# A gated linear attention with a feed-forward layer: a new order of steps, two sums moved from TensorE to VectorE, and a new layout of the feed-forward weights

## The chip, the core and the metric

The kernel runs on one core of one Trainium2 chip. The metric is the device time of one execution in microseconds (us). It is longer than the span from the first to the last instruction in the profile: 213.44 against 211.5 us for the profiled execution of the kernel before.

Ratios are computed as the mean time of one kernel's fast runs over the mean of the other's fast runs of the same rounds, on the same chip. So they are not quite the ratios of the medians that I quote. A run counts as slow here when it is over 1.5% above the fastest of its kernel; slow runs are left out of ratios.

## The reference

Four sequences of 768 tokens with 8 heads of 48 channels go through a recurrence with a decay for each channel and token. Its result, 3072 tokens of 384 features, goes through a normalised gated feed-forward layer with 1536 hidden units.

```python
for t in range(S):
    cur = np.einsum('bhd,bhe->bhde', u[None] * kt, vt)
    y[:, :, t] = np.einsum('bhd,bhde->bhe', rt, state + cur)
    state = wt[:, :, :, None] * state + np.einsum('bhd,bhe->bhde', kt, vt)
...
xn = x / rms * rms_g
g, val = xn @ w_gate, xn @ w_val
return (g * (1.0 / (1.0 + np.exp(-g))) * val) @ w_out
```

## The kernel before

The tokens are cut into six superblocks n of 128 tokens, each with four items j, one for each sequence. For each item the logarithms of the decays are summed along the tokens by a matmul with a triangular mask. The exponentials of two such sums scale r and k; then come matmuls for the scores (`q_mm`), the state (`st_mm`) and the output (`y_mm`). The feed-forward pass of superblock n (twelve steps of gate and value matmuls, then four output matmuls) is interleaved by hand with the attention of superblock n + 1. One long list, `ORDER`, gives the order of the steps. Every engine executes its share of this list in order.

```python
def cs_mm(n, j):                      # both decay sums on TensorE
    ...
    nc.tensor.matmul(a[:, NP:NP + DM]..., lhsT=mask_lt, rhs=rhs, start=True, stop=False)
    ...                               # four small matmuls: the total decay
    nc.tensor.matmul(b[:, 0:DM]..., lhsT=mask_nle, rhs=rhs, start=True, stop=True)

def st_mm(n, j):                      # the old state is added by a matmul with the identity
    old = n > 0 and n not in OLD_DVE  # OLD_DVE = () before
    if old:
        nc.tensor.matmul(ps..., lhsT=ident, rhs=st[:, n % 2, j]..., start=True, stop=False)
    for i in range(NP):
        nc.tensor.matmul(ps[:, i, :], lhsT=pair(rk[:, n % 2, j, 1], i), rhs=pair(vb[n, j], i), ...)

def load_wo(g, _):                    # one row of w_out per packet: 384 floats, cast to bf16
    ... in_=moe_w_out[...].rearrange("(c p) m -> p c m", p=128)

def fc_mm(ps, ws, n, f):              # dense slices of the gate and value weights
    for c in range(KC):
        nc.tensor.matmul(ps, lhsT=ws[:, c, f * 128:(f + 1) * 128], rhs=xnt[n][:, c, :], ...)
```

The gate matmuls and the first decay sum share two banks (`ps_a`) of PSUM, the memory that matmuls write to, the value matmuls and the second decay sum two others (`ps_b`). A matmul that needs a bank waits until its last reader is done; for `ps_b` that reader is an operation of VectorE (the multiply with k, or the product with the activated gate). In this way VectorE can hold up TensorE.

## Time and profile before

| | before |
|---|---|
| time, median of its first three runs | 212.09 us (211.61 to 215.77) |
| profiled execution | 213.44 us, span 211.5 us |
| TensorE busy | 194.5 us, 92% |
| VectorE busy | 147.6 us, 70% |
| stages 1 to 4 | 36.9, 31.8, 31.0, 28.9 us |

A stage is the stretch of the TensorE timeline from the first gate matmul of one superblock to that of the next. Before stage 1 comes a start-up of 29.3 us, after stage 4 a tail with the last two feed-forward passes. (The prediction takes the start of the fifth gate pass from the chain of waits, 158.06 us; the TensorE timeline has it at 157.90. So it gives stage 4 as 29.1 us; I use 28.9 from here on, and the tail is 53.6 us.)

### The profile page before, as it was taken

How to read it: one execution, taken by the hardware profiler on the slowest of the kernel's cores; microseconds unless marked ns; L12 is line 12 of the kernel's file. 1: busy time of each engine (PE TensorE's matmuls, PEld its weight loads, DVE VectorE, ACT ScalarE, POOL GpSimd, SP SyncE). 2: the span in 40 equal slices, each digit the busy share in tenths (PEclk: the TensorE clock that was granted, in tenths of full speed). 3: DMA queues.
4: the chain of work that ended last, by engine and by line, in shares of the span. 5: the costliest groups of instructions: out<-in, count | busy, mean ns of one | idle time of the engine just before them, and what ended most of it. 6: DMA issues, size and time to landing. Idle time of an engine off the chain costs nothing.

```text
span 211.5 us, 4381 instructions
## 1 busy us (share of the span) xinstructions
PE 194.5 (92%) x1534; PEld 107.7 (51%) x1552; DVE 147.6 (70%) x295; ACT 138.1 (65%) x282; POOL 108.6 (51%) x167
## 2 busy tenths in 40 slices
PE   5687779998998799999999999999999999999993
PEld 2455434455664245665455565455655544544563
DVE  6498744899876688988689799667886755235411
ACT  3796994769796356997546998578858873225300
POOL 3498402869597593699697889473222520000000
PEclk9999999999999999999999999999999999999999
DMA  6999999899999999999999999992177030000122
GB/s 131 217 217 183 171 203 211 169 201 168 194 205 188 190 186 228 219 213 192 192 195 222 230 222 124 236 188 48 56 186 127 20 76 20 37 0 37 40 111 76
DMA packets 126878, 32.41 MB, mean 153 GB/s; under 512 B 120580, under 2 KB 126088, under 8 KB 126856
## 3 DMA queue, kind: packets, MB, share of 16 engines
q1 hardware_dynamic: 123664, 28.58, 67.9%
q0 software_dynamic: 3184, 3.54, 10.4%
q8 instruction: 12, 0.20, 0.4%
q14 instruction: 10, 0.08, 0.1%
q10 hardware_dynamic: 8, 0.00, 0.0%
HBM read 25.96 MB, written 4.72 MB: 145 GB/s over the span
## 4 chain that ended last, share of the span: by engine, by line
PE 68%; DMA 7%; SPq 7%; DVE 6%; ACT 5%; issue 3%; POOL 3%; ACTq 0%; DVEq 0%; POOLq 0%
PE ps_b L546 20%; PE ps_a L546 19%; PE ps_q L606 18%; SPq L208 4%; DMA kt<-in_k_dram 3%; DMA vt<-in_v_dram 3%; PE ps_q L443 2%; SPq L221 2%; DMA xnt<-xn 2%; DVE ht L564 2%; PE ps_q L491 2%; PE ps_q L488 1%; DVE rk L402 1%; ACT junk L501 1%; PE ps_b L375 1%
## 5 line engine op out<-in xcount | busy, mean ns | idle before, releaser
L564 DVE TENSOR_TENSOR ht<-ps_b,sg 128x512 bf16<-128x512 f32 x72 | 48.7, 688 | 25.8 <-PE ps_b L546 18.6
L195 ACT ACTIVATE sg<-ps_a 128x512 bf16<-128x512 f32 x72 | 42.6, 596 | 36.3 <-PE ps_a L546 34.9
L546 PE MATMUL ps_b<-xnt,wv_sb 128*128 128x512 bf16 x208 | 58.6, 384 | 2.7 <-DVE rk L402 1.5
L546 PE MATMUL ps_a<-xnt,wg_sb 128*128 128x512 bf16 x206 | 58.8, 385 | 1.2 <-DVE wcol L394 0.6
L606 PE MATMUL ps_q<-wo_sb,ht 128*128 128x384 bf16 (+1 forms) x300 | 49.9, 319 | 0.0
L408 POOL TENSOR_TENSOR ruk<-rt,kt 128x384 f32<-128x384 f32 x24 | 24.3, 1011 | 25.5 <-DMA rt<-in_r_dram 20.2
L606 PEld LDWEIGHTS <-ht 128*128 128x128 bf16 x300 | 28.4, 98 | 16.9
L546 PEld LDWEIGHTS <-wv_sb 128*128 128x128 bf16 x216 | 20.2, 99 | 25.1 <-issue 4.9
L546 PEld LDWEIGHTS <-wg_sb 128*128 128x128 bf16 x216 | 20.2, 99 | 24.2 <-issue 1.7
L409 POOL TENSOR_TENSOR ruk<-ruk,u_bc 128x384 f32<-128x384 f32 x24 | 24.1, 1005 | 1.9
L418 POOL TENSOR_TENSOR ydiag<-vt,diag 128x384 f32<-128x384 f32 x24 | 19.8, 830 | 3.7 <-DVE diag L413 2.9
L461 POOL TENSOR_SCALAR_AFFINE_SELECT qts<-qts 128x512 bf16<-128x512 bf16 x20 | 12.6, 635 | 14.2 <-ACT qts L454 14.2
L450 DVE TENSOR_TENSOR qts<-ps_q,mask_lt 128x512 bf16<-128x512 f32 x24 | 16.2, 683 | 3.8 <-issue 2.5
L496 DVE TENSOR_TENSOR xb<-ps_q,ydiag 128x384 f32<-128x384 f32 x24 | 13.3, 552 | 5.3 <-PE ps_q L491 4.8
L195 ACT ACTIVATE lw<-wt 128x384 bf16<-128x384 f32 x24 | 12.0, 516 | 5.1 <-DMA wt<-in_w_dram 4.9
L514 ACT ACTIVATE xn<-xb,rstd 128x384 bf16<-128x384 f32 x24 | 14.4, 606 | 0.8 <-POOL rstd L510 0.8
L454 ACT CAST qts<-ps_q 128x512 bf16<-128x512 f32 x20 | 11.6, 584 | 4.7 <-PE ps_q L445 4.7
L501 ACT ACTIVATE junk<-xb 128x384 bf16<-128x384 f32 x24 | 12.4, 517 | 3.4 <-DVE xb L496 3.3
L402 DVE TENSOR_TENSOR rk<-kt,ps_b 128x384 bf16<-128x384 f32 x20 | 11.0, 549 | 5.1 <-ACT ps_b L195 3.0
L193 ACT ACT_TABLE_LOAD x10 | 12.8, 1283 | 1.8 <-PEq L642 1.6
L397 DVE TENSOR_TENSOR rk<-rt,ps_a 128x384 bf16<-128x384 f32 x20 | 11.0, 548 | 4.1 <-DMA rt<-in_r_dram 3.0
L615 ACT COPY ob<-ps_q 128x384 f32<-128x384 f32 (+1 forms) x12 | 5.5, 461 | 12.1 <-PE ps_q L606 11.4
(71 smaller groups left out, 271.6 us busy)
## 6 DMA issues: line engine op xcount, KB each, us to landing
wt<-in_w_dram SPq DMA_DIRECT2D x24, 192.0 KB, 3.7
vt<-in_v_dram SPq DMA_DIRECT2D x24, 192.0 KB, 4.2
kt<-in_k_dram SPq DMA_DIRECT2D x24, 192.0 KB, 3.8
rt<-in_r_dram SPq DMA_DIRECT2D x24, 192.0 KB, 3.8
out_dram<-ob SPq DMA_DIRECT2D x23, 192.0 KB, 2.8
wo_sb<-in_moe_w_out_dram POOLq DMA_DIRECT2D x3, 384.0 KB, 6.1
wv_sb<-in_moe_w_val_dram POOLq DMA_DIRECT2D x1, 768.0 KB, 10.6
wg_sb<-in_moe_w_gate_dram POOLq DMA_DIRECT2D x1, 768.0 KB, 14.0
```

Of the source, the lines that this page charges most:

```text
L195: return nc.scalar.activation(**kw).ins
L402: nc.vector.tensor_tensor(out=rk[:, n % 2, j, 1, :, 0:D], in0=inp["k", n, j], in1=bank["cs_k", n, j][:, 0:DM].rearrange("p (h d) -> p h d" ...
L408: nc.gpsimd.tensor_tensor(out=ruk[n, j], in0=inp["r", n, j], in1=inp["k", n, j], op=ALU.mult)
L409: nc.gpsimd.tensor_tensor(out=ruk[n, j], in0=ruk[n, j], in1=u_bc, op=ALU.mult)
L418: nc.gpsimd.tensor_tensor(out=ydiag[n, j], in0=inp["v", n, j], in1=diag[n, j].to_broadcast([128, H, D]), op=ALU.mult)
L450: nc.vector.tensor_tensor(out=qts[n, j][:, 0], in0=bank["q", n, j][0], in1=bc_mid(mask_lt, NP), op=ALU.mult)
L496: nc.vector.tensor_tensor(out=xb[n, j], in0=bank.pop(("y", n, j)), in1=ydiag[n, j].rearrange("p h d -> p (h d)"), op=ALU.add)
L501: nc.scalar.activation(out=junk, in_=xb[n, j], func=AF.Square, accum_out=rstd[n, j][:, 0:1])
L514: nc.scalar.activation(out=xn, in_=xb[n, j], func=AF.Copy, scale=rstd[n, j][:, 1:2])
L546: nc.tensor.matmul(ps, lhsT=ws[:, c, f * 128:(f + 1) * 128], rhs=xnt[n][:, c, :], start=(c == 0), stop=(c == KC - 1))
L564: nc.vector.tensor_tensor(out=ht[n][:, f, :], in0=bank.pop(("v", n, f)), in1=bank.pop(("sg", n, f)), op=ALU.mult)
L606: nc.tensor.matmul(ps[:, cols], lhsT=ht[n][:, f, b * L:(b + 1) * L], rhs=wo_sb[:, f, cols], start=(f == 0), stop=(f == FC - 1))
```

## The change

The intent is to take work from the fullest engine. The old state is added by VectorE in superblocks 2 to 4. The second decay sum is no longer a matmul: it is the first sum plus the logarithm itself, with the sign turned in the exponential, so one VectorE addition replaces it in superblocks 4 and 5. Each partition takes four neighbouring rows of the output weights, so that one packet carries 6144 bytes instead of 1536; the hidden units are then numbered in steps of four, and the gate and value weights are read with that stride. From superblock 1 on, the list of steps is a new one.

```diff
-    OLD_DVE = ()
+    OLD_DVE = (2, 3, 4)
+    ONE_SUM = (4, 5)
...
+        if n not in ONE_SUM:
+            nc.tensor.matmul(b[:, 0:DM]..., lhsT=mask_nle, rhs=rhs, start=True, stop=True)
+
+    def cs_add(n, j):
+        b = bank["cs_k", n, j] = psB.tile([128, 512], FP32, name="ps_b")
+        nc.vector.tensor_tensor(out=b[:, 0:DM]..., in0=bank["cs_r", n, j][:, NP:NP + DM]...,
+                                in1=lw[:, n % 2, j, :, 0:D], op=ALU.add)
...
-        act(LN_EXP, out=bank["cs_k", n, j][:, 0:DM], in_=ps, func=AF.Exp)
+        act(LN_EXP, out=bank["cs_k", n, j][:, 0:DM], in_=ps, func=AF.Exp, scale=-1.0 if n in ONE_SUM else 1.0)
...
-            in_=moe_w_out[...].rearrange("(c p) m -> p c m", p=128)
+            in_=moe_w_out[...].rearrange("(p c) m -> p c m", c=FG)
...
+    def units(ws, c, f):
+        ...
+        return ws[g][:, c, a:a + FG * 128].rearrange("p (m i) -> p i m", i=FG)[:, f % FG, :]
...
-            nc.tensor.matmul(ps, lhsT=ws[:, c, f * 128:(f + 1) * 128], rhs=xnt[n][:, c, :],
+            nc.tensor.matmul(ps, lhsT=units(ws, c, f), rhs=xnt[n][:, c, :],
...
-(ORDER: some 900 of its 1052 steps in another order)
+(ORDER: 1060 steps, the eight cs_add among them)
```

The gate and value weights also lie in one tile for each load instead of one for all, and some set-up instructions moved.

## The prediction

> **What bounds the kernel now.** I read the first page's busy shares and its 40-slice strip, then the timeline of TensorE, then the chain of work that ended last, then the timeline of VectorE. Page, busy time and strip (each digit is a fortieth, 5.3 us):
>
> ```profile
> PE 194.5 (92%) x1534; PEld 107.7 (51%) x1552; DVE 147.6 (70%) x295; ACT 138.1 (65%) x282; POOL 108.6 (51%) x167
> ...
> PE   5687779998998799999999999999999999999993
> ...
> DMA  6999999899999999999999999992177030000122
> ```
>
> TensorE is full from about 31 us to the end, apart from a dip in slice 13. The DMA engines are full until about 140 us: they fetch all inputs ahead. Which of the two sets the time has to be read stage by stage. A stage here runs from the first gate matmul of one superblock to that of the next. In the TensorE timeline the first gate matmuls stand at 29.3, 66.2, 98.0, 129.0 and 158.1 us, so stages 1 to 4 last 36.9, 31.8, 31.0 and 29.1 us; start-up is 29.3, the tail (the last two feed-forward passes) 53.4.
>
> Durations of matmuls overlap, so I take their cost from the distances between starts (timeline of TensorE: start, duration, instruction):
>
> ```profile
> 119.70 0.33 PE L370 MATMUL ps_a<-lw,mask_lt 128*128 128x384 bf16 x1
> 119.86 0.24 PE L373 MATMUL ps_a<-ones_col,lw 128*128 128x1 bf16 x4
> 119.96 0.32 PE L375 MATMUL ps_b<-lw,mask_nle 128*128 128x384 bf16 x1
> 120.12 2.11 PE L606 MATMUL ps_q<-wo_sb,ht 128*128 128x384 bf16 x12
> 122.07 0.33 PE L370 MATMUL ps_a<-lw,mask_lt 128*128 128x384 bf16 x1
> ...
> 128.29 0.32 PE L468 MATMUL ps_q<-st,ident 128*128 128x384 bf16 x1
> 128.46 0.33 PE L471 MATMUL ps_q<-vb,rk 128*128 128x96 bf16 x4
> ```
>
> The second decay-sum matmul (L375) holds the array for 120.12 - 119.96 = 0.16 us, the identity matmul that brings in the old state (L468) for 0.17, twelve output matmuls for 1.95, and the timeline gives 0.65 for three gate or value matmuls, 0.335 for the q matmuls of one item, 0.375 for the y, 0.17 for state and for the transposes of xn. Summing each stage's program order with these gives TensorE 32.4, 29.2, 30.6, 28.6 us in stages 1 to 4. The excess over the sums is 4.5, 2.6, 0.4 and 0.5: stages 3 and 4 are bound by TensorE, stage 2 has one hole. Of stage 1's excess some 2.3 us is matmuls at half pace between 30.1 and 34.1 us (0.43 each instead of 0.216), the rest small waits.
>
> The hole of stage 2, in the chain of work that ended last (start, us, what):
>
> ```profile
> 64.17 5.69 DMA kt<-in_k_dram
> 69.86 0.03 issue
> 69.89 0.02 DVEq L402
> 69.91 0.04 issue
> 69.95 0.57 DVE rk L402
> 70.52 0.04 issue
> 70.56 0.81 PE ps_b L546 x3
> ```
>
> The last k tile of superblock 2 lands at 69.9; its multiply frees a PSUM bank; the value matmul starts at 70.56. TensorE loses 1.7 us there and 0.75 just before (the r tile landed at 67.5, the gate matmul began at 68.2): 2.45 in all. Until there, DMA bandwidth bounds.
>
> VectorE timeline, where two operations of 384 columns follow without a wait:
>
> ```profile
> 126.59 0.54 DVE L397 TENSOR_TENSOR rk<-rt,ps_a 128x384 bf16<-128x384 f32 x1
> 127.05 0.55 DVE L402 TENSOR_TENSOR rk<-kt,ps_b 128x384 bf16<-128x384 f32 x1
> 127.51 1.11 DVE L536 TENSOR_TENSOR xnt<-ps_q,gT 128x384 bf16<-128x384 bf16 x2
> ```
>
> 0.55 us long, but 0.46 to 0.47 apart: VectorE overlaps them too, and its true load is below the 70% of the page. I use 0.475 for 384 columns and 0.61 for 512 (115.36 to 115.97 in the same view), 0.56 for the two state multiplies together.
>
> **What the Trainium skill says.** (1) "TensorE: Matmul & The Clock Gate", section "Back-to-back issue gap", gives the warm gap as N/2.4 + 2.5 ns: 162.5 for 384 columns. The trace agrees (1.95 us / 12 = 162.5 ns). (2) The same page, section "Weight-path perf modes", lets fast weight loads read columns packed or strided, and "SBUF — State Buffer", section "Door 1: The DMA port swizzle", says that accesses keep full bandwidth with two hits per 16-byte line. The new gate and value weights are read every fourth bf16, 8 bytes apart, so just two per line. No load of the kernel before is strided, so the trace can't confirm it. (3) "VectorE: DVE Perf Modes", section "The DRAIN you can't avoid", has the next operation wait until the pipe is empty; the starts 0.46 apart at 0.55 length show that independent operations do overlap here. (4) "DMA: Bandwidth & Descriptors", section "Why small descriptors are slow", has a fixed cost per packet. The trace's packet records agree for the weights: 768 bytes (as written) take 86 ns, 1024 take 113, 2048 take 172.
>
> **The change, part by part.**
> Old state on VectorE for superblocks 2 to 4: twelve identity matmuls go, 12 x 0.163 = 1.96 us of TensorE; twelve in-place adds of 384 columns come on VectorE, 12 x 0.475 = 5.7 us. Each add is read by the multiply right behind it, which can't overlap it, so rather 0.55 to 0.6.
> One sum for superblocks 4 and 5: eight mask matmuls go, 8 x 0.16 = 1.3 us; eight adds come, 3.8 us, and they stand between the sum and both exponentials, since the exponential of r overwrites the bank that the add reads. That chain grows by about 0.6 us.
> Output weights four rows per partition: 1536 packets of 768 written bytes become 384 of 3072. From the three sizes above I estimate 230 ns for such a packet, so 384 x 0.23 = 88 us of engine time instead of 132, over 16 engines 2.7 us of full DMA, at 41 to 55 us, which is before the hole. The price is strided weight loads: 432 of them, now 99 ns each beside matmuls 216 ns apart, so even doubled they stay hidden.
> The order: the same on TensorE up to the sixth gate matmul of the first pass. In the load queue the last k tile of superblock 2 now has one 192 KB load fewer ahead, about 1 us at the 195 GB/s of that stretch. With the 2.7 it could land 3 to 4 us earlier, so the 1.7 us wait should vanish. The 0.75 us before it may stay: fewer matmuls now stand between the last decay sum and the gate matmul that needs its bank.
>
> Sums of the new order, stage by stage, in us (TensorE before, after; VectorE before, after): stage 1: 32.4, 31.9; 26.1, 26.1. Stage 2: 29.2, 29.1; 23.7, 24.7. Stage 3: 30.6, 28.9; 24.2, 28.9. Stage 4: 28.6, 27.6; 21.5, 23.8. Stage 3 worked out for VectorE: 16 operations of 512 columns are 9.7; 35 of 384 (27 old in kind, 4 state adds, 4 sum adds) 16.6; state multiplies 2.2; small copies 0.3. There VectorE becomes as long as TensorE, and neither can be packed without gaps; it will wait for banks and TensorE will wait for it.
>
> So: start-up 29.3. Stage 1: 31.9 + the old excess of 4.5 = 36.4 (-0.5). Stage 2: 29.1 + 1.2 left of the waits = 30.3 (-1.5). Stage 3: 28.9 + 1.3 for two full engines = 30.2 (-0.8; my estimate of the gaps, about what VectorE idled in the output half of that stage before). Stage 4: 27.6 + 0.8 for the longer chain = 28.4 (-0.7). Tail 53.4, whose order hardly differs. Sum 208.0 of span against 211.5, so -3.5; the timed runs are 212.1 in the median and 211.6 at best: 208.3 expected.
>
> **The rivals.** VectorE takes the bound fully: stage 3 keeps its 31 us or grows, and stage 4's longer chain eats its saving. Then only stages 1 and 2 gain, 210 us. For it: the equal sums. Against it: stages 2 and 4 leave VectorE 4 us of room, and an order found for this mix would spread the work.
> The order also closes the small holes: all 3.3 us of TensorE work, the 2.45 us of waits and 1 us of stage 1 come back: 205 us. For it: the hole's cause is treated twice. Against it: DMA stays full up to 140 us, and the next late tile may take k's place.
> Strided weights slow TensorE: 5 ns more per matmul would be 432 x 5 = 2.2 us, giving 210.5. For it: two hits per line is the limit of what the skill allows. Against it: loads lie beside matmuls twice as long.
>
> **Range and chances.** These put most of the weight between 205.5 and 211. Two per cent faster is 207.8, just below my centre: 0.42 faster, 0.55 within, 0.03 slower.
>
> **What would show it.** No L468-like matmuls for superblocks 2 to 4, gate matmuls still 0.65 us for three; output-weight loads landing in under 5.5 us (6.1 now); no k landing in the chain near 67 us; VectorE at about 158 us busy, and waits of gate or value matmuls on VectorE around the start of the third stage's successor (125 to 128 us). Wrong would be: gate matmuls wider apart, stage 3 above 31 us, or the chain running through a DMA again in stage 2.

## The result, and the profile after

| | before | after |
|---|---|---|
| median (4 runs each) | 212.2 us | 209.45 us (209.05 to 212.91) |
| ratio of fast runs | | 0.9873 (95%: 0.9839 to 0.9907) |
| profiled execution, time and span | 213.44, 211.5 us | 209.31, 207.6 us |
| stages 1 to 4 | 36.9, 31.8, 31.0, 28.9 us | 36.2, 30.0, 30.2, 28.8 us |
| start-up, tail | 29.3, 53.6 us | 29.0, 53.4 us |

So the new kernel is faster by 1.3%, less than 2%. A second measurement (first experiment) gave 0.9932.

Page of the new kernel, busy time and the strip of 40 slices:

```profile
PE 190.4 (92%) x1515; PEld 112.2 (54%) x1532; DVE 154.8 (75%) x315; ACT 137.9 (66%) x282; POOL 109.2 (53%) x167
...
PE   5686878997999999999999999999999999999993
...
DMA  6999999999899999899899999992157110201032
```

TensorE lost 4.1 us of busy time and VectorE gained 7.2. The dip of TensorE in slice 13 (counted from 0) is gone; the weak slices after start-up are now 6 and 9 (31 to 36 and 47 to 52 us), within stage 1. The DMA strip is as full as before until 140 us.

Groups of instructions of the new kernel (line, engine, operation, output and inputs, shapes, count; busy us, mean ns of one; idle time before). The first is the addition of the old state, the second the addition that replaces the mask matmul, the third the strided load of gate weights:

```profile
L487 DVE TENSOR_TENSOR ps_q<-ps_q,st 128x384 f32<-128x384 f32 x12 | 6.7, 559 | 0.5 <-PE ps_q L481 0.4
L384 DVE TENSOR_TENSOR ps_b<-ps_a,lw 128x384 f32<-128x384 f32 x8 | 4.4, 556 | 0.1
L561 PEld LDWEIGHTS <-wg_sb 128*128 128x128 bf16 x216 | 23.5, 114 | 21.5 <-DMA wg_sb<-in_moe_w_gate_dram 1.3 <-issue 0.9 <-DVE wcol L404 0.3
```

Both additions cost what a 384-column operation of VectorE did before (0.55 us), PSUM output or not. A strided load takes 114 ns where a dense one took 99.

Start of stage 2 in the TensorE timeline of the new kernel, where the hole was:

```profile
66.51 0.81 PE L561 MATMUL ps_a<-xnt,wg_sb 128*128 128x512 bf16 x3
67.16 0.81 PE L561 MATMUL ps_b<-xnt,wv_sb 128*128 128x512 bf16 x3
67.80 0.33 PE L481 MATMUL ps_q<-vb,rk 128*128 128x96 bf16 x4
67.98 0.81 PE L561 MATMUL ps_a<-xnt,wg_sb 128*128 128x512 bf16 x3
69.13 0.23 PE L453 MATMUL ps_q<-rkT 48*128 48x128 bf16 x1 [0.34 <-DMA rkT<-rk]
```

The second gate and value matmuls follow the first at 0.65 us; no k or r tile is waited for. A transposed tile costs 0.34 us a little later. But the wait for a DMA has not left the kernel. This is the chain of work in stage 1 of the new kernel (start, us, what):

```profile
40.55 6.74 DMA rt<-in_r_dram
47.29 0.02 issue
47.31 0.57 DVE rk L407
47.88 0.05 issue
47.93 0.62 PE ps_q L435 x8
```

The r tile of the last item of superblock 1 takes 6.7 us to land. TensorE stands at the transposes that need it for 1.0 us. The kernel before comes to the same transposes one group of three gate matmuls later, and does not wait for them. Earlier in stage 1, at 36.8 us, the new kernel waits 1.15 us for gate weights; the first profile of the kernel before has no such wait.

Busy time in two windows of 10 us at the end of stage 3; columns are the stretch, its length, then TensorE, weight loads, VectorE, ScalarE and GpSimd busy with their instruction counts. Before:

```profile
110.00:120.00 10.00, 9.95 (x110) 5.64 (x110) 8.21 (x17) 7.22 (x15) 7.99 (x12) 1.00 0.99 204
120.00:130.00 10.00, 9.95 (x98) 6.53 (x96) 8.92 (x22) 8.88 (x21) 8.59 (x15) 1.00 1.11 207
```

After:

```profile
110.00:120.00 10.00, 9.92 (x101) 6.15 (x102) 9.92 (x22) 8.73 (x19) 7.70 (x13) 1.00 1.01 222
120.00:130.00 10.00, 9.51 (x78) 5.65 (x78) 9.84 (x24) 7.70 (x16) 7.93 (x12) 1.00 1.02 198
```

VectorE went from 8.2 and 8.9 to 9.9 and 9.8 us of each ten: it is now the full engine there, and TensorE has its first gaps (9.51). The VectorE timeline at the head of stage 4 of the new kernel shows who is behind whom:

```profile
126.17 0.56 DVE L487 TENSOR_TENSOR ps_q<-ps_q,st 128x384 f32<-128x384 f32 x1
126.77 0.73 DVE L489 TENSOR_TENSOR st<-ps_q,wcol 48x192 bf16<-48x192 f32 x2
127.52 0.57 DVE L487 TENSOR_TENSOR ps_q<-ps_q,st 128x384 f32<-128x384 f32 x1
128.12 0.72 DVE L489 TENSOR_TENSOR st<-ps_q,wcol 48x192 bf16<-48x192 f32 x2
128.88 1.29 DVE L579 TENSOR_TENSOR ht<-ps_b,sg 128x512 bf16<-128x512 f32 x2
```

Two additions of the old state (L487) with their multiplies (L489) stand ahead of the first two gated products (L579). Those products free the value banks, and the third value matmul starts only at 129.62, some 0.2 us late. The largest wait of stage 4 is at its end, in the TensorE timeline:

```profile
149.73 0.32 PE L373 MATMUL ps_a<-lw,mask_lt 128*128 128x384 bf16 x1 [0.44 <-DVE rk L407]
```

There a matmul of the first decay sum waits until VectorE's multiply with r has freed its bank. On VectorE the last two additions of the old state with their multiplies (145.31 to 148.0 us), an addition of the second sum (148.01) and a copy stand ahead of that multiply (149.12). Each addition of the old state is 0.60 us from the multiply that reads it, where independent operations start 0.46 to 0.47 apart.

### The profile page after: what moved, and what is told of

Same layout as the page of the kernel before. It is cut to its first block, busy times and chain, and to the rows that moved or that the text cites. A ratio compares the mean times of both kernels' runs of the same rounds, so it can differ in the third digit from the quotient of the medians.

```text
span 207.6 us, 4376 instructions
## 1 busy us (share of the span) xinstructions
PE 190.4 (92%) x1515; PEld 112.2 (54%) x1532; DVE 154.8 (75%) x315; ACT 137.9 (66%) x282; POOL 109.2 (53%) x167
## 4 chain that ended last, share of the span: by engine, by line
PE 64%; SPq 19%; DMA 8%; DVE 4%; issue 2%; ACT 1%; POOL 0%; DVEq 0%; ACTq 0%
PE ps_b L561 19%; PE ps_a L561 18%; PE ps_q L621 17%; SPq L210 15%; DMA rkT<-rk 4%; SPq L223 3%; DMA rt<-in_r_dram 3%; PE ps_q L453 3%; PE ps_q L501 2%; PE ps_q L498 2%; DMA out_dram<-ob 1%; PE ps_a L373 1%; PE ps_q L481 1%; DVE ps_b L384 1%; DVE ob L628 1%
## 5 line engine op out<-in xcount | busy, mean ns | idle before, releaser
L579 DVE TENSOR_TENSOR ht<-ps_b,sg 128x512 bf16<-128x512 f32 x72 | 48.8, 686 | 21.8 <-PE ps_b L561 15.7
L197 ACT ACTIVATE sg<-ps_a 128x512 bf16<-128x512 f32 x72 | 42.8, 596 | 29.3 <-PE ps_a L561 28.1
L561 PE MATMUL ps_b<-xnt,wv_sb 128*128 128x512 bf16 x208 | 57.9, 381 | 1.0 <-issue 0.4
L418 POOL TENSOR_TENSOR ruk<-rt,kt 128x384 f32<-128x384 f32 x24 | 24.9, 1038 | 22.5 <-DMA rt<-in_r_dram 15.5
L561 PEld LDWEIGHTS <-wg_sb 128*128 128x128 bf16 x216 | 23.5, 114 | 21.5 <-DMA wg_sb<-in_moe_w_gate_dram 1.3
L561 PEld LDWEIGHTS <-wv_sb 128*128 128x128 bf16 x216 | 23.0, 114 | 19.8 <-issue 1.3
L628 DVE COPY ob<-ps_q 128x384 f32<-128x384 f32 (+1 forms) x13 | 7.0, 536 | 8.2 <-PE ps_q L621 8.1
```

Source lines behind the costliest of these rows:

```text
L197: return nc.scalar.activation(**kw).ins
L418: nc.gpsimd.tensor_tensor(out=ruk[n, j], in0=inp["r", n, j], in1=inp["k", n, j], op=ALU.mult)
L561: nc.tensor.matmul(ps, lhsT=units(ws, c, f), rhs=xnt[n][:, c, :], start=(c == 0), stop=(c == KC - 1))
L579: nc.vector.tensor_tensor(out=ht[n][:, f, :], in0=bank.pop(("v", n, f)), in1=bank.pop(("sg", n, f)), op=ALU.mult)
```

## The experiments

All experiments had five rounds, on three chips. Each time is the median of six runs, beside eleven runs of the kernel before. The table has the ratio to the kernel before and, from each kernel's one profiled execution, that execution's time, the stages, and the sum of stages 2 to 4.

| kernel | ratio (95%) | profiled us | stage 1 | 2 | 3 | 4 | 2 to 4 |
|---|---|---|---|---|---|---|---|
| before, first profile | | 213.44 | 36.9 | 31.8 | 31.0 | 28.9 | 91.7 |
| before_again | 1.0016 (0.9962, 1.0070) | 212.03 | 35.9 | 31.1 | 30.9 | 28.9 | 91.0 |
| after, first profile | 0.9873 (0.9839, 0.9907) | 209.31 | 36.2 | 30.0 | 30.2 | 28.8 | 88.9 |
| new_again | 0.9932 (0.9888, 0.9977) | 209.90 | 37.7 | 29.6 | 30.2 | 28.8 | 88.6 |
| new_old_on_pe | 0.9921 (0.9880, 0.9962) | 209.54 | 36.0 | 30.0 | 30.6 | 28.4 | 89.0 |
| new_two_sums | 0.9968 (0.9933, 1.0003) | 211.22 | 37.0 | 30.1 | 30.7 | 29.0 | 89.9 |
| new_weights_before | 0.9942 (0.9897, 0.9987) | 211.77 | 39.1 | 29.5 | 30.1 | 28.8 | 88.4 |
| new_order_alone | 1.0007 (0.9968, 1.0045) | 211.36 | 37.7 | 30.0 | 31.1 | 28.9 | 90.0 |
| new_dense_wrong | 0.9918 (0.9872, 0.9964) | 214.17, slow | 34.1 | 29.5 | 30.2 | 28.8 | 88.4 |
| old_new_weights | 1.0007 (0.9972, 1.0042) | 211.09 | 36.1 | 30.4 | 31.0 | 29.0 | 90.4 |
| old_order_old_on_dve | 1.0079 (1.0037, 1.0121) | 211.22 | 36.1 | 29.4 | 31.5 | 30.4 | 91.3 |
| old_order_one_sum | 1.0049 (1.0003, 1.0094) | 211.92 | 35.6 | 30.6 | 32.1 | 28.9 | 91.6 |
| new_sum_alone | 0.9962 (0.9906, 1.0017) | 210.99 | 37.0 | 30.0 | 30.6 | 28.3 | 88.8 |
| try_better | 0.9949 (0.9894, 1.0004) | 210.82 | 36.8 | 30.6 | 30.5 | 28.4 | 89.5 |

The intervals are 0.3 to 0.6% wide to each side, about 1 us, so most pairs can't be told apart by time alone. Stages 3 and 4 can: the same program repeats there to 0.1 us (30.2 and 28.8 in four profiles of what is the same code for these stages but for the weights; 30.9 or 31.0 and 28.9 in both profiles of before).

**The new kernel once more.** No edit.

> The new kernel unchanged, as the mark for the three others on the same chip. Every theory: 209.3 us within 0.4, ratio to the kernel before 0.987 within 0.003; stages 1 to 4 within 0.4 us of 36.2, 30.0, 30.2 and 28.8 us. It also tells whether the half-pace stretch at the start of the first feed-forward pass (4 us long before, 1 us long after) belongs to the kernel or to the single execution.

Measured: 210.01 us, before 211.19. Time and ratio lie outside what was expected; stages 2 to 4 are as expected, stage 1 is 37.7 us and so outside. The waits of stage 1 repeat and are longer: 1.32 us for gate weights, 1.13 for VectorE, 1.53 for the r tile (1.15, 0.23 and 1.00 in the first profile). The half-pace stretch at the start of the first pass lasts until 30.5 us here, until 31.1 in the first profile of the new kernel, until 34.1 in the first profile of before, until 31.7 in its second, until 33.9 in new_old_on_pe: it belongs to the execution, not to the kernel. Where it is long (the first profile of before, new_old_on_pe, new_weights_before, try_better), TensorE doesn't wait for gate weights behind it; where it is short (both profiles of the new kernel, new_order_alone, before_again), it waits 1.1 to 1.3 us for them. What varies from run to run lies in start-up and stage 1. The ratio 0.9932 is higher than the first 0.9873; the intervals meet only at their ends, so the size of the gain is known no better than 0.7 to 1.3%.

**The old state back on TensorE.**

```diff
-    OLD_DVE = (2, 3, 4)
+    OLD_DVE = ()
```

> The new kernel with the old state back on TensorE for superblocks 2 to 4 (12 identity matmuls of 0.163 us back, 12 adds off VectorE), the order kept. Theory A, TensorE sets stages 2 to 4 and the adds are beside it: 1.6 to 2 us slower than the new kernel, 211.1 us. Rival B, VectorE sets stage 3, so that moving work to it bought nothing there: within 0.5 us of the new kernel, 209.3, with stage 3 (30.2 us) not longer.

Measured: 209.83 us against 210.01 of the new kernel in the same rounds: no slower. The twelve identity matmuls (1.96 us of TensorE) cost nothing that shows. The stages show why: stage 3 is 0.45 us longer with them (30.62 for 30.17), but stage 4 is 0.47 us shorter (28.37 for 28.84), though TensorE has two identity matmuls (0.33 us) more to do there. Both waits of the new kernel's stage 4 are gone: the one of 0.2 us at the third value matmul (VectorE comes to the first gated product at 128.37 and not at 128.88, though the stage began 0.7 us later) and the one at the stage's end, 0.6 us between starts. Rival B holds in its result; its detail (stage 3 not longer) doesn't.

**Both decay sums back on TensorE.**

```diff
-    ONE_SUM = (4, 5)
+    ONE_SUM = ()
...
     def cs_add(n, j):
+        if n not in ONE_SUM:
+            return
```

> The new kernel with both decay sums as matmuls in superblocks 4 and 5 (8 mask matmuls of 0.16 us back, 8 adds off VectorE), the order kept. Theory A: 1.0 to 1.3 us slower than the new kernel, 210.5 us. Rival B, the add's longer chain (sum, add, two exponentials) and VectorE's load eat what TensorE saves: within 0.4 us of 209.3, and the waits of TensorE at the ends of stages 3 and 4 (0.31 and 0.44 us) gone.

Measured: 210.82 us, ratio 0.9968 against 0.9932 for the new kernel. That is 0.8 us in the medians, and the intervals overlap. Stages 3 and 4 are 0.56 and 0.19 us longer. Theory A, with 0.75 us in these two stages instead of 1.0 to 1.3. The wait of 0.31 us at the end of stage 3 did not go; the one of 0.44 us at the end of stage 4 did. In new_old_on_pe both are gone: in this order the first comes with the old state alone, the second needs both moves.

**The weights as before, in the new order.**

```diff
-        return ws[g][:, c, a:a + FG * 128].rearrange("p (m i) -> p i m", i=FG)[:, f % FG, :]
+        return ws[g][:, c, a + f % FG * 128:a + (f % FG + 1) * 128]
...
-            in_=...rearrange("(p c) m -> p c m", c=FG)).ins
+            in_=...rearrange("(c p) m -> p c m", p=128)).ins
```

> The new kernel with the weights as before: output weights one row per packet again, gate and value weights read densely. Theory A, the 2 us of DMA time saved at 41 to 52 us is what lets the last k and r tiles of superblock 2 come in time: 1 to 2 us slower, 210.8 us, with a wait on a DMA of k or r at the start of stage 2 and stage 2 above 31 us. Rival B, the new order of loads alone closed that hole: within 0.4 us of 209.3. Rival C, strided weight loads (114 ns against 99) cost time on TensorE: faster by 0.5 us or more, 208.7.

Measured: 210.08 us, ratio 0.9942: no difference from the new kernel that the intervals show. The output weights land in 8.6 us instead of 5.6 (medians of three loads), and in the packet records they take 124 us of DMA engine time instead of 97. No k or r tile is waited for at the start of stage 2, which is the shortest but one of all (29.5 us). So theory A falls: the DMA saving is real, but it is not what closed the hole. The profiled execution has a long stage 1 (39.1 us, with 1.79 us of wait for the multiply with r). From 50.8 to 54.0 us the clock that the trace gives as granted to TensorE was 0.50 of full speed, and seven matmuls lost 0.21 us each. It was also the slowest but one of its six runs (211.77; the four fastest 209.5 to 210.2), so I don't read more from it.

**The new order alone.** The three edits above together.

> The new order with all three other parts undone (old state and second sum on TensorE, weights as before). Theory A, the parts add up (TensorE 3.3 us, DMA 1 to 2): 212 to 214 us, no faster than the kernel before. Rival B, the order is what closed the holes and the rest is traded between engines: 209.5 to 210.5 us.

Measured: 211.89 us, before 211.72, ratio 1.0007. Theory A: the order by itself gains nothing in time. It has no hole at the start of stage 2 (stage 2 is 30.0 us), but TensorE waits 1.59 us in stage 1, and stage 2 begins at 66.3 us, as late as before (66.2 and 65.6). Stages 3 and 4 are as long as before (31.1 and 28.9). The wait is at the same transposes as in the new kernel, but not for the r tile: its load was issued at 40.51 and landed 4.1 us later. It is the multiply with r on VectorE that lasts 2.45 us instead of 0.56. The timelines of TensorE, VectorE and GpSimd:

```profile
48.92 0.62 PE L437 MATMUL ps_q<-ident,rk 128*128 128x128 bf16 x8 [1.59 <-DVE rk L409]
...
46.41 2.45 DVE L409 TENSOR_TENSOR rk<-rt,er 128x384 bf16<-128x384 f32 x1
...
46.83 0.65 POOL L473 TENSOR_SCALAR_AFFINE_SELECT qts<-qts 128x512 bf16<-128x512 bf16 x1
47.44 1.00 POOL L420 TENSOR_TENSOR ruk<-rt,kt 128x384 f32<-128x384 f32 x1
```

In superblock 1 both inputs of the multiplies with r and k lie in SBUF, the core's main on-chip memory; in the other superblocks one input lies in PSUM. Over the fourteen profiles the former take 0.54 to 0.56 us where GpSimd is idle and up to 2.45 us where it works beside them; the latter never take more than 0.56 us. So GpSimd is the likely cause; no run moved its operations alone.

**The new weights alone, in the old order.** The edits of the diff for `load_wo`, `units` and `fc_mm`, on the kernel before.

> The kernel before, with the new weights alone (four rows per partition, strided reads). Theory A, the hole at the start of stage 2 comes from full DMA engines and shrinks by what they save, 2.2 us (132 to 97 us over 16 engines): 1 to 2.2 us faster, 210.5 us, the k tile landing at 67 to 68 us and not 69.9. Rival B, the saving comes too early or is refilled by other loads: within 0.5 us of 212.1.

Measured: 212.22 us, ratio 1.0007. The hole is smaller in this profile: the value matmul waits 0.95 us (0.80 in the record), and the k tile has landed by 67.0 us. But the time does not change. Rival B.

**The old state on VectorE, in the old order.**

```diff
-    OLD_DVE = ()
+    OLD_DVE = (2, 3, 4)
```

> The kernel before, in its own order, with the old state added on VectorE in superblocks 2 to 4. Theory A, TensorE bounds stages 2 to 4: 1.5 to 2 us faster, 210.4 us. Rival B, in an order not made for it VectorE's 6.7 us more delay the multiplies that free the banks: within 0.5 us of 212.1 or slower.

Measured: 213.21 us, ratio 1.0079: slower by 0.8%, with the whole interval above 1. TensorE has 1.96 us less to do, and stages 3 and 4 grow by 0.5 and 1.5 us. The TensorE timeline of this kernel names the waits, one in each stage:

```profile
111.33 0.81 PE L546 MATMUL ps_b<-xnt,wv_sb 128*128 128x512 bf16 x3 [0.83 <-DVE ht L564]
...
130.70 0.81 PE L546 MATMUL ps_b<-xnt,wv_sb 128*128 128x512 bf16 x3 [0.94 <-DVE ht L564]
```

Each time a value matmul waits for a gated product that VectorE reaches late, in stage 3 behind one addition with its state multiplies and three other operations, in stage 4 behind two additions with theirs. Stage 4 has a further wait at its end, 0.52 us for a multiply with r. Rival B, and more than it said.

**Dense gate and value weights with the new output weights.** Its output is wrong, which doesn't matter for the time.

```diff
-        return ws[g][:, c, a:a + FG * 128].rearrange("p (m i) -> p i m", i=FG)[:, f % FG, :]
+        return ws[g][:, c, a + f % FG * 128:a + (f % FG + 1) * 128]
```

> The new kernel with gate and value weights read densely while the output weights stay four rows per partition: a wrong result on purpose, for it pairs the hidden units wrongly. It measures the stride alone. Theory A, strided loads stay hidden beside the 216 ns matmuls: within 0.4 us of the new kernel, 209.3, load duration back from 114 to 99 ns. Rival C: 0.5 to 2 us faster.

Measured: 210.7 us in the median with one slow run, ratio 0.9918 against 0.9932 for the new kernel (of other rounds, on another chip). The load takes 98 ns again. The profiled execution was slow, with a wait of 6.9 us in start-up, so I use only its stages 3 and 4: 30.15 and 28.77 us against 30.17 and 28.84. The stride is hidden, theory A.

**The kernel before once more.** No edit.

> The kernel before, unchanged, profiled a second time. Its first profile is of an execution of 213.44 us, slower than its median. Theory A, the 2.45 us hole at the start of stage 2 belongs to the kernel: the hole is there again at 2 us or more, stage 2 31.5 to 32 us. Rival B, the hole's size belongs to that execution: the execution takes about 211 us, the hole is 1.5 us or less; stages 3 and 4 are 31.0 and 28.9 us as before within 0.1. Ratio 1.000 within 0.003 in either case.

Measured: 212.0 us, ratio 1.0016. The profiled execution took 212.03 us, 1.4 less than the first. The start of its stage 2:

```profile
67.12 0.82 PE L546 MATMUL ps_a<-xnt,wg_sb 128*128 128x512 bf16 x3
...
69.22 0.81 PE L546 MATMUL ps_b<-xnt,wv_sb 128*128 128x512 bf16 x3 [1.28 <-DVE rk L402]
```

The gate matmul starts 0.23 us late, the value matmul 1.45: a hole of 1.7 us, not 2.45. It lies between the two theories: the hole belongs to the old order, its size to the execution. In the five profiles in the old order it is 2.45, 1.7, about 1, about 1, and none; in the nine profiles in the new order the k tile is never waited for there.

**The single sum alone, in the new order.** The new kernel with `OLD_DVE = ()` and the weights as before.

> The new order with the single decay sum alone (old state on TensorE, weights as before). Theory A, the sum on VectorE in the order made for it is the one part that pays: as fast as the whole new kernel, ratio 0.992 to 0.994 to the kernel before, stage 3 30.6 us and stage 4 28.4 us as with the old state on TensorE. Rival B, all three parts are needed: 0.997 or more.

Measured: 210.72 us, before 212.1, ratio 0.9962; the interval reaches from theory A (0.992 to 0.994) beyond rival B (0.997), so the time decides nothing. The stages do: 30.6 and 28.3 us. Against the new order alone that is 0.50 and 0.66 us less, 1.16 of the 1.3 us that the eight mask matmuls cost. The sum of stages 2 to 4 (88.8 us) is that of the whole new kernel (88.9 and 88.6).

**The single sum in the old order.** The edits for `cs_mm`, `cs_add` and `exp_k` on the kernel before, with each `cs_add` ahead of the first exponential.

> The kernel before in its own order, with the single decay sum added on VectorE for superblocks 4 and 5 just ahead of the first exponential. Theory A, the new order is needed to absorb the adds: ratio 1.00 or above, stages 3 and 4 no shorter than 31.0 and 28.9 us. Rival B, the sum pays by itself: about 1 us faster, 0.995, each of stages 3 and 4 0.4 us shorter.

Measured: 212.55 us, ratio 1.0049: not faster, and just slower by its interval. Stage 3 is 1.2 us longer than before (32.1), with TensorE waiting 0.53 us for ScalarE and 0.59 us for VectorE at its end; stage 4 is unchanged. Theory A.

**A try at something faster.** The old state on VectorE in superblocks 2 and 3 only, the single sum also in superblock 3, and the second gate load ahead of the second value load.

```diff
-    OLD_DVE = (2, 3, 4)
-    ONE_SUM = (4, 5)
+    OLD_DVE = (2, 3)
+    ONE_SUM = (3, 4, 5)
(ORDER: cs_add.3.0 to cs_add.3.3 ahead of the first exponential of their item;
 load_gv.1.0 and load_gv.1.1 change places)
```

> A try at a faster version: the new kernel with the old state on VectorE only in superblocks 2 and 3 (its adds at the head of stage 4 held up the multiplies), the single sum also in superblock 3 (stage 2 has VectorE time to spare), and the second gate load issued ahead of the second value load. If the stages hold what the traces say: stage 1 0.5 us shorter (the 1.2 us wait on the gate weights halved or gone), stage 2 0.3 to 0.6 us shorter, stages 3 and 4 together 0.1 to 0.3 us shorter: 1 us faster than the new kernel, 208.5 to 209 us, ratio 0.988. Rival: the adds at the end of stage 2 cost as much as they save, and stage 1 is set by the r tile anyway: equal to the new kernel, 0.993.

Measured: 210.7 us, ratio 0.9949: the new kernel is not beaten. Of its three parts, the change of loads shows nothing: the gate weights are not waited for, but neither are they in new_old_on_pe and new_weights_before, which have the old order of loads and as long a half-pace stretch (to about 33.9 us in all three). Stage 1 is 36.8 us, with 1.56 us of wait for the multiply with r, whose tile had landed at 44.0. The sum in superblock 3 made stage 2 longer, 30.6 us, with TensorE waiting 0.67 us for VectorE:

```profile
94.11 0.32 PE L274 MATMUL ps_a<-lw,mask_lt 128*128 128x384 bf16 x1 [0.67 <-DVE wcol L305]
```

The old state in fewer superblocks does what new_old_on_pe suggested: stages 3 and 4 come to 58.83 us together against 59.01 (30.45 + 28.38, 30.17 + 28.84), 0.2 us.

## Why the prediction was right or wrong

The time, 209.45 us, lies in the range, and the kernel is faster by less than 2%, the likeliest of the three outcomes. The predicted gain was 3.8 us; measured were 2.75 (difference of the medians) and, in the second measurement, 1.2. So the predicted gain was too large.

**What bounds.** Right for stages 3 and 4. TensorE is the bound there before, to 0.5 us of the sum of its work.

**The sum over stages.** Right in size. Predicted for start-up, stages and tail: 29.3, 36.4, 30.3, 30.2, 28.4, 53.4, together 208.0 us. Measured: 29.0, 36.2, 30.0, 30.2, 28.8, 53.4, together 207.6. For stage 1 this is luck. I carried over the old excess of 4.5 us, of which 2.3 were the half-pace stretch of that execution. In the new kernel's profile that stretch costs 1.0 us, and waits for gate weights (1.15) and for the r tile (1.0), which I hadn't foreseen, fill the difference. In stage 2 the 0.75 us that I had left standing went too, and a wait of 0.34 us for a transposed tile came.

**From the span to the time.** This step was mis-sized: "the timed runs are 212.1 in the median and 211.6 at best: 208.3 expected". The profile that I worked from belongs to an execution of 213.44 us. Its span of 211.5 us corresponds to that time, not to the median. With the 1.7 to 1.9 us between span and time, 208.0 us of span is 209.8 us, which is 0.35 from the measured median. Working from an execution slower than the median also made the gain too large: the hole that the change should close was 2.45 us in that execution and 1.7 us in the second one.

**The hole of stage 2.** That it would close was right. Its cause was not. I gave 2.7 us of it to the output weights and 1 us to the order of loads. The saving of DMA time was 2.2 us (132 to 97 us of engine time over 16 engines; a packet takes 253 ns, not 230), and 1.7 against the second profile of the kernel before, where the same packets take 124 us. With the weights as before the hole stays closed (new_weights_before), and with the new weights alone the time doesn't change (old_new_weights). The order closes it, and alone it gains nothing (new_order_alone): what it saves at the start of stage 2 it loses in stage 1.

In eight of the nine profiles of the new order, all but the slow one (0.26 us), TensorE waits 1.0 to 1.8 us for the last multiply with r of superblock 1; in the five of the old order it never does. In two of the eight (both of the new kernel) VectorE waits for the tile, which lands at 47.3 and 48.2 us: the rival's "the next late tile may take k's place", though it is r's, and earlier. In the other six the tile had landed by 45.0 us, 1.3 to 3.5 us before the multiply began, and the multiply took 1.3 to 2.45 us, with GpSimd at work beside it. No term of the prediction stands for that. The load steps ahead of this tile are the same in both orders, but TensorE comes to the transposes one group of gate matmuls sooner. That the DMA engines' throughput sets the arrival of the tile, where it is late, is likely, as they are full from 5 to 140 us, but no run varied it alone.

**VectorE becomes as full as TensorE in stage 3.** Right: 9.92 and 9.84 us of ten, and 1.2 us between stage 3 (30.15) and the sum of TensorE's work there (28.9), where I had put 1.3. Sums by the same costs for the other programs of the new order (an estimate) say whose it is: the excess is 0.5 us with neither move, 0.6 with the sum alone, 1.1 with the old state alone. So most of it comes with the old state.

**The parts.** The prediction took the old state and the sum as equal in kind, TensorE time saved minus gaps. The sum pays almost its full price, 1.16 of 1.3 us, and only in the order made for it. The old state pays nothing: it gains 0.45 us in stage 3 and gives 0.47 back in stage 4. In stage 3 TensorE is spared six identity matmuls (0.98 us), and the stage is shorter by less than half of that. I had charged stage 4 with 0.8 us "for the longer chain" of the sum. The excess there is 28.84 - 27.6 = 1.2 us, and the sum by itself is not enough for it: with the sum alone stage 4 is 28.3 us, 0.3 above its own sum of work. Of what the state additions bring, 0.2 us is lost at the head of the stage and 0.6 at its end, where they and the longer chain stand in one queue on VectorE; that second wait goes when either move is undone.

**The order.** The first rival had it that "an order found for this mix would spread the work". That is shown: the same two moves in the old order, the second in the one place tried, cost 0.8% and 0.5%.

**Strided loads.** Right: 114 ns instead of 99, and hidden. But the full bandwidth that I took from "SBUF — State Buffer" for two hits per line doesn't show: such a load is 15 ns longer.

**The gap between matmuls.** The section "Back-to-back issue gap" that I cited gives its formula for an isolated matmul, which I left out. These traces have its 162.5 ns in a stream of twelve.

**The signs.** VectorE busy was to be about 158 us and is 154.8: the page's busy time counts overlapped time once, so added operations of 0.55 us show as less. Output-weight loads under 5.5 us to landing was wrong: 6.4 and, the second time, 5.6. Waits on VectorE around 125 to 128 us are there (0.31 us at 125.31, then the third value matmul).

What stays open: why the gain was 1.3% in one measurement and 0.7% in the next, and whether stage 1 would be shorter if GpSimd's operations moved away from the multiplies of superblock 1, or if these read PSUM.

## What to carry to other kernels

Moving work from the fullest engine to the next pays only where the receiver isn't on the way to the buffers that the giver waits for. Look at what stands behind the new operation in the receiver's queue, and count the receiver's load stage by stage, not over the whole kernel. Work from a profile whose execution time is close to the median, or compare two profiles of the same kernel before trusting a hole's size. When a wait disappears, look at the stage's starting time, not only at the place: here the time was lost again earlier. And when a wait names an operation of another engine, look at that operation's duration and at when its inputs landed, before you blame a load.

## What the Trainium skill lacked or had wrong

- "VectorE: DVE Perf Modes", section "The DRAIN you can't avoid": it says that the next operation waits for an empty pipe, and then that one which is not held starts earlier. (That section gives no size; another page of the skill does.) In these runs independent operations of 384 columns, 0.55 us long, start 0.46 to 0.47 us apart; one that reads the result of the operation before it starts 0.60 us after it. So a sum of durations overstates VectorE's load, for such operations by some 15%.
- "TensorE: Matmul & The Clock Gate", section "Weight-path perf modes": it allows strided reads in a fast load and gives no duration for them. Here a load of 128 columns, 8 bytes apart, took 114 ns, a dense one 98 to 99.
- "DMA: Bandwidth & Descriptors": I found no packet durations for loads that cast from 4 to 2 bytes. Here packets of 768, 1024, 2048 and 3072 written bytes took 80 to 86, 99 to 113, 172 and 252 to 261 ns.
